# One program order for the experts of the first mixture: layers interleaved, VectorE's flags last

## The chip, the cores and the metric

The kernel runs on one core of one Trainium2 chip. The metric is device time in microseconds (us), median of the runs of a version. TensorE (PE) multiplies, VectorE (DVE) and ScalarE (ACT) do elementwise work, GpSimd (POOL) issues gathers and scatters through a table of row numbers, and SyncE (SP) issues the other transfers.

## The reference

What is computed is an attention without softmax, then two mixtures of experts (MoE), on 4608 rows of 512:

```python
kv = np.einsum('bhsd,bhse->bhde', k, v)
out = np.einsum('bhsd,bhde->bhse', q, kv)        # then a norm over each head
...
for e in range(E):                               # MoE1: 8 experts, two per row
    for k in range(2):
        mask = top2[:, k] == e
        h = np.maximum(x[mask] @ w1[e], 0.0)
        out[mask] += top2_w[mask, k, None] * (h @ w2[e])
...
do_compute = x @ w_skip > 0                      # MoE2: one expert per kept row
logits = x[do_compute] @ w_gate
...
out[do_compute] = xc + gate_w * (np.maximum(xc @ w1[e], 0.0) @ w2[e])
```

## The kernel before

Products are made from 16-bit halves: a matrix in 32 bits is scaled by a power of two and split into a high and a low part, and three products of parts stand for one.

The attention and the routing of MoE1 end some 240 us into the span. Then come the experts of MoE1. Each expert has ten tiles of 128 rows (a tile of row numbers each), and two tiles make a group, so an expert has five groups; two groups of expert 0 are done earlier, and 38 are left. Here a **slot** is the work of PE between the ends of two groups. A group is layer 1 in four pieces of 24 products (line 218, out to `hh` by ACT and `hl` by DVE, lines 226 and 227) and layer 2 for each tile (line 252, 24 products each, out to `ysb` by ACT, line 1010). The last group of an expert has 224 rows instead of 256.

A tile's result is added to the result of the row's other expert (`yo`, gathered by POOL from `ydram`, line 1001; the sum is line 1014) and scattered to `out_dram` (line 1017). It also goes into the routing of MoE2: squares (`jk`, line 867), a power of two from them, two parts (`xh`, lines 870 and 871), a transposing transfer (`x2T`, line 886), products with the gate (lines 891 and 893), some twenty small operations of DVE, ranks (lines 934 to 936), and a product that puts the row's number into its place in MoE2's tables (line 964).

Beside this, the weights of the next expert and those of MoE2 are prepared. The table `MATS` has five letters per expert, one per group: F is half of the next expert's weights (`wa`, `wb`), P is half of an expert's weights of MoE2 (`presplit`, which is then written to `wsd` in DRAM, line 1036). A matrix of 2 MB is loaded into one of two `stage` buffers (lines 187, 191), squared in four passes (`wjunk`, line 165), its sums reduced (`wsum`, line 168) and added over partitions on PE (line 171), a power of two made from it, and then split in four parts, each by ACT (line 181) and DVE (line 182).

PE's order is written by hand throughout. From group 3 to group 34 the order of the other four engines is set by the framework's scheduler, which takes instructions by its own estimate of when they are ready; before and after they run as the program is written. All DMAs that SP issues go through one queue.

After group 37 come units of MoE2: `Ra[0]`, `Ra[1]` (two units whose rows are known early) and u0, u1 and so on, whose rows come from `next_rows`, after the last group's place.

Of the kernel before, what the change touches and what calls it, by code (L numbers as in the profile page):

```python
# [15 lines left out]
P = 128  # L16
# [15 lines left out]
BEGIN = 3  # L32
# [3 lines left out]
AHEAD = [{(CUT + 2, 0): "g", (CUT + 2, 1): "a", (CUT + 3, 0): "s", (CUT + 3, 1): "b"},  # L36
         {(CUT + 3, 2): "g", (CUT + 4, 0): "s", (CUT + 4, 1): "a"}]
# [41 lines left out]
def moe_kernel(ctx: ExitStack, tc: tile.TileContext, q, k, v, g_norm, w_gate, w_noise, noise,  # L79
# [43 lines left out]
    def pow2_scale(ss_ps, kk, name):  # L123
# [5 lines left out]
        V.tensor_scalar(u[:, 0], t, -1.0, float(kk), op0=ALU.mult, op1=ALU.add)  # L129
        V.tensor_scalar(u[:, 1], t, 1.0, float(254 - kk), op0=ALU.mult, op1=ALU.add)  # L130
        s = tiny.tile([P, 2, n], I32, name=name + "s")
        V.tensor_scalar(s, u, 23, None, op0=ALU.logical_shift_left)  # L132
        f = s.bitcast(F32)
        return f[:, 0], f[:, 1]
# [21 lines left out]
    def split_matrix(load, hi, lo, scale, kk, sc, inv):  # L156
# [15 lines left out]
        a0, i0 = pow2_scale(ps, kk, "wsc")  # L172
        if scale is None:
            V.tensor_copy(sc, a0)  # L174
        else:
            V.tensor_mul(sc, a0, scale)
        V.tensor_copy(inv, i0)
# [53 lines left out]

    def layer1(W, xT, nt, point=None):
        hh = p2.tile([P, 8, 2 * P], F16, name="hh")
        hl = p2.tile([P, 8, 2 * P], F16, name="hl")
        if nt % P:
            G.memset(hh[:, :, nt:2 * P], 0.0)
            G.memset(hl[:, :, nt:2 * P], 0.0)
        for fp in range(8 * nt // 512 if nt % P == 0 else 4):
            layer1_piece(W, xT, nt, hh, hl, fp)
            if point:  # L240
                point(fp)
        return hh, hl
# [583 lines left out]


# [3 lines left out]
    racc = m1.tile([P, 1], F32, name="racc")  # L831
    rjunk = m1.tile([P, 36], F32, name="rjunk")
    A.activation(rjunk, rw.rearrange("p c n -> p (c n)"), AF.Square, accum_out=racc)
    rps = pSm[0].tile([P, 1], F32, name="small")
    PE.matmul(rps, ones32, racc, start=True, stop=True)
    rs, ri = pow2_scale(rps, 199, "rsc")
    rsk = m1.tile([P, 2], F32, name="rsk")
    V.tensor_copy(rsk[:, 0:1], rs)
    V.tensor_copy(rsk[:, 1:2], ri)
# [734 lines left out]
```

## Time and profile before

| | us |
|---|---|
| median of three runs | 1341.67 (1341.3 to 1344.72) |
| profiled execution, its time | 1338.29 |
| its span | 1336.3 |
| attention and routing, to the first slot | 243.0 |
| 38 slots of MoE1 | 243.0 to 1098.8 |
| MoE2 and the end | 1098.8 to 1336.3 |

PE is busy for 1220.6 us of the span (91%), DVE for 799.7, ACT for 667.3. The mean granted clock is 0.969. A slot can be read as a stretch of PE between the last products of one group's layer 2 and those of the next; a view that cuts the span at these ends gives each slot's length, every engine's busy time in it, the granted clock and how busy the DMA engines were.

### The profile page before, as it was taken

What the parts mean: (1) busy time and instruction counts of PE and PEld (TensorE: products, weight loads), DVE (VectorE), ACT (ScalarE), POOL (GpSimd) and SP (SyncE); (2) the same over time, 40 slices, a digit from 0 to 9 for tenths busy, and PEclk for the clock granted to TensorE, in tenths of its full rate; (3) what the DMA queues carried; (4) which work ended last, traced back from release to release, by engine and by line L of the source; (5) the groups of instructions that cost most, each with busy time, mean ns of one, the idle gap of its engine ahead of it and who ended that gap; (6) DMA issues with size and microseconds to landing.
All of it is one profiled execution on the core that took longest, in us unless ns stands there. A gap on an engine that the chain in (4) does not pass through costs nothing.

```text
span 1336.3 us, 25221 instructions
## 1 busy us (share of the span) xinstructions
PE 1220.6 (91%) x9443; PEld 866.1 (65%) x9443; DVE 799.7 (60%) x2730; ACT 667.3 (50%) x1227; POOL 388.3 (29%) x460
## 2 busy tenths in 40 slices
PE   5777789898999999999999999999999999999995
PEld 5666677565667666756666666666576766576663
DVE  1667878134585776676667766667776765433321
ACT  1569662255565656476466575647574332122210
POOL 2322332212333232423332232242312342222220
PEclk8978889998999999999999999999999999999998
DMA  9989963667985977888799797778977584677670
GB/s 239 294 241 297 310 181 86 176 196 220 262 236 164 258 259 196 238 208 266 153 287 264 255 292 242 225 202 265 304 232 225 150 211 137 198 243 224 197 225 13
DMA packets 318757, 296.30 MB, mean 222 GB/s; under 512 B 211888, under 2 KB 263088, under 8 KB 314524
## 3 DMA queue, kind: packets, MB, share of 16 engines
q1 hardware_dynamic: 294940, 210.31, 58.3%
q0 software_dynamic: 23104, 83.18, 18.5%
q8 instruction: 78, 1.28, 0.4%
q10 hardware_dynamic: 576, 1.05, 0.3%
q14 instruction: 59, 0.48, 0.1%
HBM read 174.46 MB, written 94.73 MB: 201 GB/s over the span
## 4 chain that ended last, share of the span: by engine, by line
PE 34%; DVE 19%; issue 15%; ACT 13%; DMA 12%; POOL 4%; SPq 2%; POOLq 0%; DVEq 0%; ACTq 0%
PE b L252 18%; PE a L218 10%; DMA stage<-in_moe_w_dram 8%; ACT wjunk L165 3%; DVE wb L182 2%; ACT presplit L181 2%; DVE wa L182 2%; DVE hl L227 2%; DMA xg<-xrows,idx 2%; DVE xh L871 2%; PE kvps L385 1%; PE b L450 1%; ACT hh L226 1%; ACT ysb L1010 1%; POOL out_dram L1096 1%
## 5 line engine op out<-in xcount | busy, mean ns | idle before, releaser
L218 PEld LDWEIGHTS <-wa 128*128 128x128 f16 x5184 | 474.4, 99 | 68.1 <-issue 15.4
L218 PE MATMUL a<-xT,wa 128*128 128x256 f16 (+1 forms) x3648 | 403.9, 271 | 12.9 <-DVE hl L227 10.6
L252 PE MATMUL b<-wb,hh 128*128 128x512 f16 x1536 | 352.6, 380 | 19.8 <-ACT hh L226 19.7
L252 PEld LDWEIGHTS <-hh 128*128 128x128 f16 x1536 | 144.2, 98 | 188.6 <-ACT hh L226 34.0
L226 ACT ACTIVATE hh<-a 128x512 f16<-128x512 f32 (+1 forms) x192 | 109.9, 577 | 191.1 <-PE a L218 190.8
L1017 POOL DMA_INDIRECT out_dram<-x,oi x70 | 73.1, 1045 | 430.2 <-DVE nact L946 308.2
L252 PE MATMUL b<-wb,hl 128*128 128x512 f16 x768 | 182.6, 380 | 1.9 <-DVE hl L227 1.9
L227 DVE SCALAR_TENSOR_TENSOR hl<-a,hh 128x512 f16<-128x512 f32 (+1 forms) x192 | 128.0, 674 | 77.0 <-ACT hh L226 76.9
L252 PEld LDWEIGHTS <-hl 128*128 128x128 f16 x768 | 75.2, 98 | 94.0 <-DVE hl L227 4.1
L1010 ACT ACTIVATE ysb<-b,gate 128x512 f32<-128x512 f32 x76 | 51.7, 680 | 154.3 <-PE b L252 154.3
L165 ACT ACTIVATE wjunk<-stage 128x1024 bf16<-128x1024 f32 x96 | 101.0, 1052 | 38.0 <-DMA stage<-in_moe_w_dram 36.8
L218 PE MATMUL a<-x2Tr,wa 128*128 128x256 f16 (+1 forms) x1152 | 109.2, 257 | 4.9 <-DMA x2Tr<-xh 4.5
L978 POOL DMA_INDIRECT xg<-xrows,idx x76 | 75.2, 990 | 97.3 <-DVE gate L987 58.4
L1001 POOL DMA_INDIRECT yo<-ydram,gi x70 | 77.1, 1101 | 60.9 <-issue 21.5
L182 DVE SCALAR_TENSOR_TENSOR presplit<-stage,wscl,presplit 128x1024 f16<-128x1024 f32 x64 | 80.0, 1279 | 9.5 <-ACT presplit L181 9.0
L181 ACT ACTIVATE presplit<-stage,wscl 128x1024 f16<-128x1024 f32 x64 | 70.7, 1139 | 15.3 <-DVE wscl L174 15.3
L450 PE MATMUL b<-kvbd,qTs 128*128 128x160 f32 x256 | 52.8, 346 | 21.8 <-issue 10.0
L1014 DVE TENSOR_TENSOR x<-ysb,yo 128x512 f32<-128x512 f32 x70 | 48.2, 689 | 34.5 <-ACT ysb L1010 33.6
L867 ACT ACTIVATE jk<-x 128x512 bf16<-128x512 f32 x70 | 43.9, 627 | 45.3 <-DVE x L1014 44.7
L494 POOL TENSOR_TENSOR osb<-osb,rinv 128x1024 f32<-128x1024 f32 (+1 forms) x20 | 37.2, 1862 | 86.9 <-DVE rinv L141 71.6
L450 PEld LDWEIGHTS b<-kvbd,qTs 128*128 128x128 f32 x256 | 42.7, 219 | 26.5 <-issue 10.8
L870 ACT ACTIVATE xh<-x,x2ss 128x512 f16<-128x512 f32 x70 | 46.7, 714 | 18.7 <-DVE x2ss L132 18.0
(330 smaller groups left out, 1510.6 us busy)
## 6 DMA issues: line engine op xcount, KB each, us to landing
stage<-in_moe_w_dram SPq DMA_DIRECT2D x32, 2048.0 KB, 10.4
ydram<-ysb SPq DMA_DIRECT2D x66, 256.0 KB, 5.6
wsd<-presplit SPq DMA_DIRECT2D x8, 2056.0 KB, 7.2
wsd<-presplit SPq DMA_DIRECT2D x8, 2048.0 KB, 8.9
out_dram<-zeros SPq DMA_DIRECT2D x9, 1024.0 KB, 8.1
km<-in_k_dram SPq DMA_DIRECT2D x16, 512.0 KB, 7.0
vm<-in_v_dram SPq DMA_DIRECT2D x16, 512.0 KB, 6.3
qm<-in_q_dram SPq DMA_DIRECT2D x16, 512.0 KB, 7.3
```

The source lines that it names most:

```text
L165: A.activation(junk, st[:, F * c:F * c + F], AF.Square, accum_out=acc[:, c:c + 1], **kw)
L181: A.activation(hi[:, d], st[:, d], AF.Copy, scale=sc)
L182: V.scalar_tensor_tensor(lo[:, d], st[:, d], sc, hi[:, d], op0=ALU.mult, op1=ALU.subtract)
L218: PE.matmul(ps[:, i, :], a[:, c, fs], xT[:, b + c, 0:nt], start=(n == 0), stop=(n == 11))
L226: A.activation(hh[:, fsl, 0:nt], ps, AF.Relu)
L227: V.scalar_tensor_tensor(hl[:, fsl, 0:nt], ps, 0.0, hh[:, fsl, 0:nt], op0=ALU.max, op1=ALU.subtract)
L252: PE.matmul(ps, a[:, f, gsl], b[:, f, :], start=(fs.start == 0 and i == 0), stop=(fs.stop == 8 and a is hl and f == 7))
L450: PE.matmul(po[:, i, :], qT[:, i, :], kvb[b % 4][:, h0 + i, :], start=True, stop=True)
L978: G.indirect_dma_start(out=xg[:, g], out_offset=None, in_=xrows, in_offset=bass.IndirectOffsetOnAxis(ap=idx1[:, t0 + g:t0 + g + 1], axis=0))
L1001: G.indirect_dma_start(out=yo, out_offset=None, in_=ydram[0:e * C1, :], in_offset=bass.IndirectOffsetOnAxis(ap=gi[:, g:g + 1], axis=0), bo ...
L1010: A.activation(ysb, ps, AF.Copy, scale=gate[:, g:g + 1])
L1017: s = G.indirect_dma_start(out=out, out_offset=bass.IndirectOffsetOnAxis(ap=oi[:, g:g + 1], axis=0), in_=x2[:, g], in_offset=None, bounds_ ...
```

## The change

All engines run in program order from the first slot on, and the program is written anew for it as a slot per group. Layer 1 of the next group now stands between the two halves of layer 2 of this group: two pieces, layer 2 of the first tile, two pieces, layer 2 of the second tile. The steps of the routing and of the matrices have fixed places. A matrix is loaded at the end of one slot, squared in the next and split in the one after. The flags and the gate column of a group (from its gathered rows) stand last on DVE in the slot ahead. The squares and powers of two of the second gate are made per tile instead of per group. `pow2_scale` takes three operations of DVE instead of four and writes its results where they are wanted, several other small operations go away, and the product `rhs` moves from POOL to DVE. The layer 1 of `Ra[0]` and `Ra[1]` are done in and right behind the last slot, group 37's place follows the layer 2 of `Ra[0]`, and `others` stands ahead of the splitting of u0's rows. A fallback for overfull experts at the program's end is put inside another conditional block.

```diff
+    def pow2_scale(ss_ps, kk, name, a=None, inv=None):
...
-        u = tiny.tile([P, 2, n], I32, name=name + "u")
...
+            a, inv = f[:, 0], f[:, 1]
+        V.tensor_scalar(a.bitcast(I32), t, -2.0 ** 23, kk * 2.0 ** 23, op0=ALU.mult, op1=ALU.add)
+        V.tensor_scalar(inv.bitcast(I32), t, 2.0 ** 23, (254 - kk) * 2.0 ** 23, op0=ALU.mult, op1=ALU.add)
+        return a, inv
     def log_recip_newton(r, vv, shape, name, half):
...
+    order.enter_context(tc.manual_schedule(engines={
+        mybir.EngineType.SP, mybir.EngineType.Pool, mybir.EngineType.Activation, mybir.EngineType.DVE}))
...
+        def squares(self, g, x2):
+            self.ss = tiny.tile([P, 1], F32, name="ss2")
+            jk = p2.tile([P, D], BF16, name="jk", bufs=1)
+            A.activation(jk, x2, AF.Square, accum_out=self.ss)
+            self.a = tiny.tile([P, 1], F32, name="x2a")
+            pow2_scale(self.ss, 195, "x2s", self.a, self.rsc[:, g:g + 1])
+        def parts(self, g, x2):
+            xh = self.xh
+            A.activation(xh[:, g, 0:D], x2, AF.Copy, scale=self.a)
+            V.scalar_tensor_tensor(xh[:, g, D:2 * D], x2, self.a, xh[:, g, 0:D], op0=ALU.mult, op1=ALU.subtract)
+            SP.dma_start_transpose(out=self.xT[:, :, g * P:g * P + P], in_=xh[:, g])
...
+        def flags(self):
+            aux = self.xg[:, :, 512:528]
+            e = self.e
+            if e:
+                self.fl = tiny.tile([P, 2], F32, name="fl")
+                V.tensor_scalar(self.fl, aux[:, :, 8], float(e), None, op0=ALU.is_equal)
+                nf = tiny.tile([P, 2], F32, name="nf")
+                V.tensor_scalar(nf, self.fl, -BIG, BIG, op0=ALU.mult, op1=ALU.add)
+                self.gi = tiny.tile([P, 2], I32, name="gi")
+                V.tensor_add(self.gi, aux[:, :, 9], nf)
+                self.oi = tiny.tile([P, 2], I32, name="oi")
+                V.scalar_tensor_tensor(self.oi, idx1[:, self.t0:self.t0 + 2], -1.0, nf, op0=ALU.add, op1=ALU.add)
+            self.gate = tiny.tile([P, 2], F32, name="gate")
+            V.tensor_scalar(self.gate, aux[:, :, e], Ws[e][4], None, op0=ALU.mult)
...
+        def out(self, g):
+            e = self.e
             ysb = p2.tile([P, D], F32, name="ysb", bufs=3)
-            A.activation(ysb, ps, AF.Copy, scale=gate[:, g:g + 1])
+            A.activation(ysb, self.ps, AF.Copy, scale=self.gate[:, g:g + 1])
             if e < E - 1:
-                SP.dma_start(ydram[(t0 + g) * P:(t0 + g + 1) * P, :], ysb)
+                SP.dma_start(ydram[(self.t0 + g) * P:(self.t0 + g + 1) * P, :], ysb)
             if e:
...
+    def matrix(n):
+        m = mats[n] if n < len(mats) else None
         if m is None:
             return None
         kind, e, half = m
         if half == 0:
             gens[kind] = first_weights(e, w1, w2, gcol, 0.5, Ws[e]) if kind == "first" else presplit(e)
-        return gens[kind][half]
-    engines = {mybir.EngineType.SP, mybir.EngineType.Pool, mybir.EngineType.Activation, mybir.EngineType.DVE}
-    begin = ExitStack()
-    begin.enter_context(tc.manual_schedule(engines=engines))
-    xs = {0: gather1(*groups[0])}
+        g = gens[kind][half]
+        next(g)
+        return g
...
+    def go(g, n=1):
+        for _ in range(n if g else 0):
+            next(g, None)
+    for g in groups[0:3]:
+        g.gather()
     for t in yob:
...
+    for g in groups[0:2]:
+        g.turn()
+    groups[0].flags()
+    squares = matrix(0)
+    parts = None
+    l1 = groups[0].first()
+    for i in range(4):
+        l1.matmuls()
+        l1.out()
+    prev = prev2 = Nothing()
+    for n, cur in enumerate(groups):
...
+        h = l1.h
+        l1 = groups[n + 1].first() if n + 1 < len(groups) else Layer1(Wa[0], Ra[0].xT, 2 * P)
+        l1.matmuls()
+        prev.out(1)
+        cur.others()
+        prev.scatter(1)
+        prev.squares(1)
+        l1.out()
+        l1.matmuls()
+        prev.parts(1)
+        if n + 2 < len(groups):
+            groups[n + 2].turn()
+        go(parts)
+        l1.out()
+        prev2.then("ranks")
+        cur.second(0, h)
+        go(parts)
+        prev2.then("slots")
+        go(squares)
+        go(parts)
+        go(squares)
+        ahead_work(n, 0)
+        l1.matmuls()
+        cur.out(0)
+        cur.scatter(0)
+        cur.squares(0)
+        l1.out()
+        l1.matmuls()
+        cur.parts(0)
+        ahead_work(n, 1)
+        l1.out()
+        go(parts)
+        prev2.then("place")
+        prev.then("logits")
+        cur.second(1, h)
+        if n == CUT + 2:
+            pick_early()
+        go(parts)
+        prev.then("gate")
+        ahead_work(n, 2)
+        go(squares, 2)
+        after = matrix(n + 1)
+        if n == 0:
+            prepare()
+        if n + 3 < len(groups):
+            groups[n + 3].gather()
+        if n + 1 < len(groups):
+            groups[n + 1].flags()
+        prev, prev2 = cur, prev
+        parts, squares = squares, after
+    l1s = [l1, Layer1(Wa[1], Ra[1].xT, 2 * P)]
+    l1 = l1s[1]
+    l1.matmuls()
+    prev.out(1)
+    prev.scatter(1)
+    prev.squares(1)
+    l1.out()
+    l1.matmuls()
+    prev.parts(1)
+    prev2.then("ranks")
+    prev2.then("slots")
+    l1.out()
+    for i in range(2):
+        l1.matmuls()
+        l1.out()
+    prev2.then("place")
...
+    def step(k):
+        if k == 0:
+            prev.then("logits")
+            prev.then("gate")
+        elif k == 1:
+            prev.then("ranks")
+            prev.then("slots")
+        else:
+            prev.then("place")
+            next_rows()
+            for _ in range(2):
+                stream.pop(0).gather(osc2)
+    moe2_unit(Wa[0], Ra[0], step, h=l1s[0].h)
+    def step(k, f=later(-1)):
+        if k == 1:
+            others()
+            f(0)
+        if k:
+            f(k)
+    moe2_unit(Wa[1], Ra[1], step, h=l1s[1].h)
     for u in range(len(units)):
...
-    with flag(NX // 2):
...
+        with flag(NX // 2):
```

Three engines at the places that matter follow, each as the order of instructions before and then after.

ACT before, in the second slot of expert 2 (`wa` is the split of next weights, `wjunk` the squares of the matrix loaded meanwhile, `rdf` the exponential of the gate):

```order
L867 ACTIVATE jk,ss_5298<-x_5140 128x512
L226 ACTIVATE hh<-a 128x512
L870 ACTIVATE xh<-x_5140,x2ss 128x512 x2
L181 ACTIVATE wa<-stage,wscl 128x1024
L226 ACTIVATE hh<-a 128x512
L181 ACTIVATE wa<-stage,wscl 128x1024 x2
L226 ACTIVATE hh<-a 128x512
L181 ACTIVATE wa<-stage,wscl 128x1024
L165 ACTIVATE wjunk,wacc<-stage 128x1024
L226 ACTIVATE hh<-a 128x512
L165 ACTIVATE wjunk,wacc<-stage 128x1024 x3
L1010 ACTIVATE ysb<-b,gate 128x512
```

ACT after, from the middle of the same slot to its end:

```order
L177 ACTIVATE wa<-stage,wscl 128x1024
L164 ACTIVATE wjunk,wacc<-stage 128x1024
L177 ACTIVATE wa<-stage,wscl 128x1024
L164 ACTIVATE wjunk,wacc<-stage 128x1024
L1074 ACTIVATE ysb<-b,gate 128x512
L908 ACTIVATE jk,ss_5548<-x_5397 128x512
L222 ACTIVATE hh<-a 128x512
L914 ACTIVATE xh<-x_5397,x2a 128x512
L222 ACTIVATE hh<-a 128x512
L177 ACTIVATE wa<-stage,wscl 128x1024 x2
L941 ACTIVATE rdf<-rdf 128x16
L164 ACTIVATE wjunk,wacc<-stage 128x1024 x2
```

The four squares stood behind the four splits and ran in one go; now two stand between the first splits, and two behind the last splits and the exponential.

SP before, about the first slot of expert 2 (`wsd` is the write of a split matrix of MoE2, `stage` a load, `x2T` and `xT` transposing transfers):

```order
L1012 DMA ydram<-ysb 128x512 x2
L886 DMA_TRANSPOSE x2T<-xh 128x8x128 x2
L980 DMA_TRANSPOSE xT<-xg 128x8x128 x2
L1036 DMA wsd_2801<-presplit 128x8192
L1012 DMA ydram<-ysb 128x512
L191 DMA stage<-in_moe_w_dram 128x8x512
L1012 DMA ydram<-ysb 128x512
L886 DMA_TRANSPOSE x2T<-xh 128x8x128 x2
```

SP after, at the end of that slot:

```order
L1037 DMA_TRANSPOSE xT<-xg 128x8x128 x2
L1076 DMA ydram<-ysb 128x512
L916 DMA_TRANSPOSE x2T<-xh 128x8x128
L1113 DMA wsd_2792<-presplit 128x8192
L187 DMA stage<-in_moe_w_dram 128x8x512
L1076 DMA ydram<-ysb 128x512
L916 DMA_TRANSPOSE x2T<-xh 128x8x128
L1037 DMA_TRANSPOSE xT<-xg 128x8x128 x2
L1076 DMA ydram<-ysb 128x512
L916 DMA_TRANSPOSE x2T<-xh 128x8x128
```

The load stood behind the write and a `ydram` write; now it stands right behind the `wsd` write, at the end of the slot, with a slot's transfers behind both. Such a pair, write and load, stands at ten places of SP's order.

PE before, in a slot with a matrix (line 218 is layer 1):

```order
L218 LDWEIGHTS wa
L218 MATMUL a<-xT,wa 128x256
L218 LDWEIGHTS wa
L218 MATMUL a<-xT,wa 128x256
L171 MATMUL small<-wsum,ones_72 128x1
L218 LDWEIGHTS wa
L218 MATMUL a<-xT,wa 128x256
L218 LDWEIGHTS wa
L218 MATMUL a<-xT,wa 128x256
```

PE after, in such a slot (line 264 is layer 2; lines 978 to 980 are ranks):

```order
L214 LDWEIGHTS wa
L214 MATMUL a<-xT,wa 128x256
L170 MATMUL small<-wsum,ones_72 128x1
L978 LDWEIGHTS tri_74
L978 MATMUL small<-rm_4085,tri_74 128x16
L979 LDWEIGHTS ones_70
L979 MATMUL small<-rm_4085,ones_70 128x8
L980 LDWEIGHTS ones_70
L980 MATMUL small<-c_2810,ones_70 128x16
L264 LDWEIGHTS hh
L264 MATMUL b<-wb,hh 128x512
L264 LDWEIGHTS hh
```

The sum of the squares was added between two pieces of layer 1; now it stands behind the slot's second piece, ahead of layer 2 of the first tile.

## Rows read from the trace of the kernel before

**Rows 1.** The page's chain that ended last, by line:

```profile
PE b L252 18%; PE a L218 10%; DMA stage<-in_moe_w_dram 8%; ACT wjunk L165 3%; DVE wb L182 2%; ACT presplit L181 2%; DVE wa L182 2%; DVE hl L227 2%; DMA xg<-xrows,idx 2%; DVE xh L871 2%; PE kvps L385 1%; PE b L450 1%; ACT hh L226 1%; ACT ysb L1010 1%; POOL out_dram L1096 1%
```

**Rows 2.** Slots: bounds, length, busy PE, PEld, DVE, ACT, POOL, clock, DMA share, GB/s.

```profile
407.90:428.20 20.30, 20.28 (x169) 14.45 (x166) 10.78 (x49) 10.50 (x21) 5.02 (x6) 1.00 0.55 122
428.20:449.80 21.60, 21.60 (x171) 14.87 (x170) 15.78 (x58) 10.57 (x17) 9.51 (x9) 1.00 0.85 201
...
807.00:832.70 25.70, 23.48 (x172) 15.61 (x171) 16.30 (x59) 14.48 (x25) 6.24 (x7) 0.93 0.70 227
...
sum 855.80, PE 818.42 PEld 558.20 DVE 558.59 ACT 486.68 POOL 257.29; mean PE 21.54 PEld 14.69 DVE 14.70 ACT 12.81 POOL 6.77
```

**Rows 3.** Groups on PE, 235 to 1130 us: count, busy and mean, idle before, releaser.

```profile
L218 PE MATMUL a<-xT,wa 128*128 128x256 f16 (+1 forms) x3648 | 403.9, 271 | 12.9 <-DVE hl L227 10.6 <-DMA xT<-xg 2.1
L252 PE MATMUL b<-wb,hh 128*128 128x512 f16 x1248 | 286.5, 379 | 17.6 <-ACT hh L226 17.5
...
L171 PE MATMUL small<-wsum,ones 128*128 128x1 f32 x60 | 9.0, 218 | 6.7 <-DVE wsum L168 6.7
```

**Rows 4.** Groups on ACT, 340 to 1100 us, same columns.

```profile
L165 ACT ACTIVATE wjunk<-stage 128x1024 bf16<-128x1024 f32 x84 | 88.4, 1053 | 37.8 <-DMA stage<-in_moe_w_dram 36.8
L226 ACT ACTIVATE hh<-a 128x512 f16<-128x512 f32 (+1 forms) x136 | 77.0, 572 | 19.8 <-PE a L218 19.6
L181 ACT ACTIVATE presplit<-stage,wscl 128x1024 f16<-128x1024 f32 x60 | 66.3, 1139 | 9.1 <-DVE wscl L174 9.1
L1010 ACT ACTIVATE ysb<-b,gate 128x512 f32<-128x512 f32 x69 | 46.9, 680 | 133.8 <-PE b L252 133.8
...
L165 ACT ACTIVATION_READ_ACCUMULATOR wjunk<-stage 128x1 f32 x84 | 16.0, 190 | 0.0
```

**Rows 5.** Groups on DVE, 340 to 1100 us, same columns.

```profile
L182 DVE SCALAR_TENSOR_TENSOR presplit<-stage,wscl,presplit 128x1024 f16<-128x1024 f32 x60 | 75.0, 1279 | 8.0 <-ACT presplit L181 7.5
...
L1014 DVE TENSOR_TENSOR x<-ysb,yo 128x512 f32<-128x512 f32 x69 | 47.5, 689 | 32.1 <-ACT ysb L1010 31.2 <-issue 0.3
```

**Rows 6.** SP's timeline, 824 to 900 us: start, duration, what.

```profile
825.18 0.33 SPq L1036 DMA_DIRECT2D wsd<-presplit  x1
...
892.09 0.53 SPq L1036 DMA_DIRECT2D wsd<-presplit  x1
```

**Rows 7.** DMAs issued from 828.3 to 828.9 us, with us to landing.

```profile
stage<-in_moe_w_dram SPq DMA_DIRECT2D x1, 2048.0 KB, 12.8
```

**Rows 8.** DMAs issued from 893.8 to 894.4 us, with us to landing.

```profile
stage<-in_moe_w_dram SPq DMA_DIRECT2D x1, 2048.0 KB, 16.1
```

**Rows 9.** The tile of loads, 340 to 1100 us, its transfers.

```profile
DMA to landing us min/median/max: 8.0/10.7/16.1
```

**Rows 10.** The written matrices, 340 to 1100 us, their transfers.

```profile
DMA to landing us min/median/max: 6.7/8.2/9.0
```

**Rows 11.** POOL's timeline at the start of expert 7, idle time before in brackets.

```profile
1000.09 1.07 POOL L1001 DMA_INDIRECT yo<-ydram,gi  x1 [6.82 <-DMA x2T<-xh]
```

**Rows 12.** PE's timeline from MoE1 into MoE2, same columns.

```profile
1123.24 0.30 PE L964 MATMUL idx2ps<-rhs,ohp 128*128 128x160 f16 x2
...
1136.21 1.89 PE L252 MATMUL b<-wb,hh 128*128 128x512 f16 x4 [2.19 <-ACT hh L226]
...
1145.57 10.64 PE L218 MATMUL a<-x2Tr,wa 128*128 128x256 f16 x96
...
1168.85 1.36 PE L218 MATMUL a<-x2Tr,wa 128*128 128x256 f16 x11 [2.28 <-DMA x2Tr<-xh]
```

**Rows 13.** Chain of waits, 1100 to 1180 us: start, us, what.

```profile
1135.70 0.75 DVE xh L871
...
1142.10 0.20 DVE tot L1356
```

**Rows 14.** Instructions of the last conditional's check, line 1427.

```profile
L1427 POOLq TENSOR_LOAD <-fli x2: 307/404/500, 1321.2 to 1326.6; - x2
```

**Rows 15.** Instructions of the program's end, line 1570.

```profile
L1570 POOLq DRAIN  x3: 40/107/5377, 1330.0 to 1336.0; - x3
```

More of the change, by code (lines that the diff above doesn't have):

```diff
@@ L1021, in moe1_group, with scatter @@
-            step(1 + g)
-            point(4 + 2 * g)
-            point(5 + 2 * g)
-        return finalize(e, i0, xg, x2, fl) if e else None
+                V.tensor_add(self.x2[:, g], ysb, yob[(self.t0 + g) % 4])
+        def scatter(self, g):
+            if not self.e:
+                return
+            G.memset(spacer, 0.0)
+            s = G.indirect_dma_start(out=out, out_offset=bass.IndirectOffsetOnAxis(ap=self.oi[:, g:g + 1], axis=0),
+                                     in_=self.x2[:, g], in_offset=None, bounds_check=N - 1, oob_is_err=False)
+            nodep(s.ins, osc + rd2, "rows of other tokens")
+            osc.append(s.ins)
@@ L1026, in presplit, with squares, parts, then @@
+        def squares(self, g):
+            if self.e:
+                if g == 0:
+                    self.fin = Finish(self.e, self.i0, self.fl)
+                self.fin.squares(g, self.x2[:, g])
+        def parts(self, g):
+            if self.e:
+                self.fin.parts(g, self.x2[:, g])
+        def then(self, what):
+            if self.e:
+                getattr(self.fin, what)()
     def presplit(e):
@@ L1168, in pick_early @@
             ahead.append(cols)
-    groups = [(e, i0) for e in range(E) for i0 in range(0, T1, 2)][EARLY // 2:]
     Ws = {0: W0}
+    groups = [Group(e, i0) for e in range(E) for i0 in range(0, T1, 2)][EARLY // 2:]
     mats = list(MATS[EARLY // 2:])
@@ L1198, in moe_kernel, with __getattr__ @@
+    class Nothing:
+        def __getattr__(self, name):
+            return lambda *a: None
+    Ra, Wa = [], ([], [])
+    NF0 = (T1 - EARLY) // 2
+    def go(g, n=1):
[3 more added lines that the diff above has]
+        g.gather()
     for t in yob:
         G.memset(t, 0.0)
[L1200 to L1242 removed]
@@ L1375, in split @@
             r.split()
-    def point(p):
-        if p == 0:
-            next(fin, None)
-            next_rows()
-            for _ in range(2):
-                stream.pop(0).gather(osc2)
-        elif p == PB:
-            split(-1)
     def later(u):
@@ new lines, in moe_kernel @@
+                sec = Second(1, p3.tile([P, 8, 2 * P], F16, name="x2Tr"))
+                sec.squares(0, xg[:, 0:D])
+                sec.parts(0, xg[:, 0:D])
+                sec.logits()
+                act, oh, gt = sec.gates(one)
+                g = tiny.tile([P, 2], F32, name="gate")
+                V.tensor_mul(g[:, 0:1], act, gt)
+                V.tensor_scalar(xg[:, D:D + 8], oh[:, 0], g[:, 0:1], None, op0=ALU.mult)
+                SP.dma_start(x2d[bass.ds(j, P), :], xg[:, 0:D + 8])
```

489 lines of the change are left out of this document (213 added, 276 removed).

## The prediction

> **What bounds the kernel now.** I read three views in this order. The page's chain shows which work ended last: products of the two layers lead (18% and 10%), and right behind them stands the load of a matrix into `stage` (8%) with the squares and splits that hang on it [rows 1]. So TensorE bounds MoE1, and what stops it comes from ACT, DVE and the loads. The slot view then says how much that is. A slot in which nothing is late takes 21.6 us and PE is busy in all of it; one of the 224-row groups takes 20.3 [rows 2]. Thirty slots of 21.6 and eight of 20.3 make 810.4 us, and the 38 slots take 855.8: **45.4 us** above an undisturbed run. The groups on PE say where PE stood: 17.6 us ahead of layer 2 for the last `hh` of its own layer 1, 12.9 ahead of layer 1 (10.6 for `hl`, which frees the buffers), 6.7 at the sum of a matrix's squares [rows 3]: 37.2 us. The other 8 or so are PE busy, but at the low clock: the slot at 807 holds a stall of 2.2 us (25.70 less 23.48 busy), its granted clock is 0.93, and PE is busy in it for 23.48 us instead of 21.6, so a stall of this size costs another 1.9.
>
> DMA engines are busy for about half of a light slot (0.55) and 0.85 of the undisturbed full one [rows 2]: they are no bound, but a transfer has to wait its turn.
>
> **What the change takes away.** In the new order a whole tile of layer 2 (5.2 us) and two later pieces stand between a piece of layer 1 and the layer 2 that reads it. The 17.6 us for `hh` are covered by that; a late `hh` has to be later than some 5 us to show again. The sums of squares are made a slot before PE asks, and the flags no longer stand ahead of DVE work that PE waits for. I take the whole 45.4 us away as the most there is: a slot cannot go below 21.6, since no product is removed.
>
> The smaller DVE edits (one power-of-two operation less, copies gone, `rhs` moved from POOL) I cost at nothing: DVE is busy for 15.8 of 21.6 us even in a slot without stalls [rows 2], so these operations lie beside PE. Without that cover, two fewer per slot at some 0.2 us and one more `rhs` are worth less than 0.5 us either way, on work that ends a slot early.
>
> **What it adds: a ring through load, squares and split.** Times are counted from the start of a slot of 21.6 us. A piece of layer 1 takes 10.64/4 = 2.66 us [rows 12], so the fourth piece ends at 5.3 + 5.2 + 5.3 + 0.3 = 16.1. Behind it ACT has the relu (0.57), then the last two splits (1.14 each), and DVE ends its half of the last one 1.28 later [rows 4, 5]: 20.3. Only then is the `stage` buffer free and the split matrix whole, and SP issues the write to `wsd` and, right behind it, the load. With T from the write's issue to the load's landing, the load lands at 20.3 + T - 21.6 = T - 1.3 of the next slot. ACT meets it there at the first square, with all its later work queued behind: three splits, `ysb`, two squares of rows, two relus, `xh`, the exponential, three squares. In a row that is four squares with their readout (4 x 1.24), three splits (3.4), five passes over 512 columns of 0.57 to 0.68 (3.2), DVE's addition (0.69), DVE's last split (1.28) and some six small operations of 0.19 (1.2): 14.7 us [rows 4, 5]. PE asks for the sum at 21.6 + 5.3 = 26.9. So **PE waits T - 1.3 + 14.7 - 26.9 = T - 13.5 us**, at the ten places where a write stands right ahead of a load. Without a write the load lands after 8.0 us at best and 10.7 in the median [rows 9], and PE waits for nothing.
>
> T is not in the trace as such. The nearest rows are loads that followed a write after 2 to 3 us: 825.18 to 828.3 + 12.8 = 841.1, that is 15.9, and 892.09 to 893.8 + 16.1 = 909.9, that is 17.8 [rows 6 to 8]; of six such loads these are the earliest and the second latest. From below, the fastest write and the fastest load one after the other make 6.7 + 8.0 = 14.7 [rows 9, 10], and if they overlap in part, 13.5 or less and no wait. By SP's order two transposing transfers stood just ahead of the write then and 256 KB of `ydram` between; in the new order neither is there. I take T = 15.5, a little under the lower row, and keep 13.5 and 17.8 as ends.
>
> The Trainium skill ("DMA: Bandwidth & Descriptors", section "Queues, rings and completion order") says that SP owns one ring on each of the DMA engines and that descriptors in a ring are consumed in order. By that the load does not start until the write's descriptors are through, and T is a sum; the landings of 15.9 and 17.8 against 10.7 agree. Were the two served side by side, T would be 10.7 and none of the ten places would wait.
>
> So with T = 15.5: ten waits of 2.0 us make 20. A wait of 2.2 brought the low clock [rows 2]; at 2.0 I count a third of 1.9, 0.6 each: 6. Five of the places (in experts 4 to 6, where such slots follow each other closely) begin with splits already late by about 1: 5.5. At the start of experts 5 and 7, POOL's gather of `yo` waits for a `ydram` write that stands in SP's queue behind the pair, and the addition, two relus and two splits behind it wait too. At expert 7 of before POOL stood 6.8 us there [rows 11], under cover; I count 2 each, 4 (0 to 8).
>
> **Around it.** `pick_early` comes last in its slot on DVE, and its slot's ranks wait: 2. At the **transition**, group 37's place came at 1123.24 and u0 started at 1145.57 without waiting [rows 12]; from the place to u0's split was 13.2 us (1136.45), and `others` took till 1142.3, some 5 us behind it [rows 13]. In the new order `others` stands ahead of the split, so u0's rows are there 16 to 21 us behind the place, while PE has only the second layer of `Ra[1]` in between, 10.4 us. PE waits 6 to 10 and pays 2 of clock. In return go the stalls of 2.19 and 2.28 with their slow clock [rows 12], about 8 together. Net -1 to +8; I take 2.6. At the **end**, POOL reads a second flag from 1326.6 and jumps, and the last drain starts at 1330.0 [rows 14, 15]. With the fallback inside the other block, check and jump go: -3.4.
>
> **The sum.** 1338.3 (profiled execution) - 45.4 + 20 + 6 + 5.5 + 4 + 2 + 2.6 - 3.4 = 1329.6. The median of the runs lies 3.4 above the profiled one: **1333 us**.
>
> **Rivals.** *Waits hidden*: write and load overlap, T is at or under 13.5. The 35.5 us of the ring are gone and the median is some 1298 to 1308 with a few small stalls left. For it speaks that the queue is emptier there; against it that none of the six loads behind a write landed so early. *The ring eats the gain (slower)*: the same mechanism with T as the rows have it. At T = 16.9, their middle, each of ten waits is 3.4, and 1.9 of clock comes with each: 53; the late splits of the close places 8, `yo` 5; 66 in place of 35.5, so 1363; at 17.8 it is 9 more for the waits and some 6 for the close places, 1378. It decides from about T = 16.2, where 2.7 + 0.7 at ten places and 10 beside them make up for all that was removed. For it speak both rows, against it the emptier queue. *It does not do what it says*: with four engines in a fixed order, small waits on DVE or ACT take the place of those removed and slots stay at 22.5; then the median is within a few us of 1341. Against it: only 15.8 us of DVE and 10.6 of ACT are busy in a slot at 21.6 [rows 2].
>
> **Chances.** About 0.3% (4 us) is what a measurement of this kernel can tell from no change. Forecast (1320 to 1344): 0.42, of which 0.33 is faster by more than that and 0.09 within it. Waits hidden: 0.20, faster. The ring eats the gain: 0.31, slower. It does not do what it says: 0.07, 0.06 of it the same, 0.01 slower. Faster 0.53, same 0.15, slower 0.32. The range leaves out half of the hidden case and a third of the slower one: **1303 to 1364**.
>
> **What would show it.** Right: idle time ahead of layer 2 for `hh` gone; most slots 21.6; waits of 1 to 3 us at the product of `wsum` two slots behind each of the ten pairs, and the chain there through load, `wjunk`, splits and `wjunk` again; loads behind a write landing 15 to 16 us after the write's issue, about 14 into a slot; a wait ahead of u0's layer 1; a POOL without second flag load. Wrong: loads landing under 13 or over 17; waits at `hl` or the rows' logits instead; slots without a write that are longer than 22.

## The result, and the profile after

The changed kernel takes **1357.1 us** (median of six runs, 1352.1 to 1367.2), the kernel before 1344.6 beside it (1341.3 to 1347.8): ratio **1.011**, 95% interval 1.008 to 1.014. The time lies inside the range of the prediction, but the forecast was faster, and the kernel is slower by 1.1%. The profiled execution took 1365.6 us (span 1363.7), 8.5 above the median; a second one, below, lies 4.8 under the median of its own run.

The page's chain of the changed kernel by line, which answers to [rows 1]:

```profile
PE b L264 17%; PE a L214 16%; DMA stage<-in_moe_w_dram 10%; DMA x2T<-xh 4%; ACT wjunk L164 3%; DVE presplit L178 3%; ACT hh L222 2%; PE b L462 1%; ACT presplit L177 1%; PE kvps L397 1%; DVE wa L178 1%; POOL out_dram L1174 1%; DMA ydram<-ysb 1%; DVE x L1078 1%; ACT xh L914 1%
```

`hh`, `wb` and `hl` no longer stand near its head; the load has grown, and `x2T` (the transposing load that brings a slot's rows to the second gate) is new, with 4%.

To see where the time is, I cut both spans at the same four points of TensorE's program: the last sum of the first routing, the first product of u0, the last product, the end. Windows of the kernel before (bounds, length, busy PE, PEld, DVE, ACT, POOL, clock, DMA share, GB/s):

```profile
0.00:240.54 240.54, 187.78 (x1539) 162.62 (x1540) 159.74 (x407) 131.75 (x293) 75.42 (x93) 0.89 0.85 234
240.54:1145.57 905.03, 863.14 (x6561) 587.72 (x6560) 586.79 (x2180) 498.16 (x860) 267.77 (x296) 0.99 0.79 225
1145.57:1319.90 174.33, 169.67 (x1345) 115.78 (x1343) 52.45 (x142) 37.42 (x74) 44.13 (x72) 0.99 0.67 206
1319.90:1336.30 16.40, 0.00 (x0) 0.00 (x0) 0.75 (x1) 0.00 (x0) 0.98 (x1) 0.62 0.05 14
```

And of the changed kernel:

```profile
0.00:246.65 246.65, 193.53 (x1539) 166.16 (x1540) 158.60 (x393) 131.35 (x291) 76.19 (x93) 0.87 0.85 233
246.65:1176.75 930.10, 867.36 (x6561) 592.10 (x6560) 600.45 (x2099) 500.44 (x862) 255.38 (x328) 0.97 0.84 219
1176.75:1350.60 173.85, 170.21 (x1344) 116.13 (x1344) 49.63 (x127) 37.08 (x74) 41.85 (x68) 0.99 0.65 203
1350.60:1363.70 13.10, 0.00 (x1) 0.00 (x0) 0.75 (x1) 0.00 (x0) 0.98 (x1) 0.69 0.04 13
```

Differences: +6.1 up to the first mixture (3.4 of it a wait for `hhe` at 239, 1.7 the slow products behind it, the rest spread over the attention), **+25.1** in it, -0.5 behind it, -3.3 at the end. The products are the same (6561 in the stretch of the mixture); 20.9 of the 25.1 are PE standing idle and 4.2 a lower clock. The groups on PE in that stretch up to 1141 us say for whom, as [rows 3] did before (count, busy and mean, idle before, releaser):

```profile
L214 PE MATMUL a<-xT,wa 128*128 128x256 f16 (+1 forms) x3648 | 400.1, 270 | 0.0
L264 PE MATMUL b<-wb,hh 128*128 128x512 f16 x1216 | 288.1, 392 | 0.0
...
L924 PE MATMUL small<-rw,x2T 128*128 128x18 f16 x272 | 16.0, 172 | 38.7 <-DMA x2T<-xh 38.7
...
L170 PE MATMUL small<-wsum,ones 128*128 128x1 f32 x60 | 9.5, 228 | 13.0 <-DVE wsum L167 13.0
L978 PE MATMUL small<-rm,tri 128*128 128x16 f16 x33 | 5.6, 170 | 3.7 <-DVE rm L966 3.7
```

Everything that [rows 3] showed ahead of both layers is gone. What is new stands at three products: the second gate's logits for `x2T`, 38.7 us; the sums of squares, 13.0; the ranks, 3.7. Five of the waits on PE's timeline, the last of them at u0 (start, duration, idle before in brackets):

```profile
729.19 0.28 PE L924 MATMUL small<-rw,x2T 128*128 128x18 f16 x4 [3.73 <-DMA x2T<-xh]
...
958.64 0.26 PE L924 MATMUL small<-rw,x2T 128*128 128x18 f16 x4 [4.03 <-DMA x2T<-xh]
...
1016.87 0.38 PE L170 MATMUL small<-wsum,ones 128*128 128x1 f32 x2 [2.56 <-DVE wsum L167]
...
1103.93 0.28 PE L924 MATMUL small<-rw,x2T 128*128 128x18 f16 x4 [26.92 <-DMA x2T<-xh]
...
1176.75 3.59 PE L214 MATMUL a<-x2Tr,wa 128*128 128x256 f16 x16 [7.33 <-DMA x2Tr<-xh]
```

The fourth alone is 26.9 us, more than the whole difference in the mixture (25.1). The changed kernel's chain of waits names the transfer, and, in the first row, an ordinary load behind a write:

```profile
987.30 14.15 DMA stage<-in_moe_w_dram
...
1070.06 33.83 DMA x2T<-xh
```

SP's timeline: a write and a load, then, at the long wait, `x2T` of slot 36, then `x2Tr` (the transposing load of the first row unit):

```profile
986.92 0.33 SPq L1113 DMA_DIRECT2D wsd<-presplit  x1
987.30 0.46 SPq L187 DMA_DIRECT2D stage<-in_moe_w_dram  x1
...
1070.06 1.33 SPq L916 DMA_TRANSPOSE x2T<-xh  x1
1075.22 31.60 SPq L1158 DMA_TRANSPOSE x2Tr<-xh  x2
```

And POOL's, which gathers the two halves of the first row unit's weights, 2 MB each:

```profile
1065.42 0.97 POOL L1124 DMA_INDIRECT wa<-wsd,ewi  x1 [0.30 <-PE small L980]
...
1071.24 0.97 POOL L1124 DMA_INDIRECT wb<-wsd,ewi  x1 [0.30 <-issue]
```

`x2T` was issued between the two gathers, and the two instructions of `x2Tr` behind it kept SP for 31.6 us (the first alone for 19.2). What the DMA engines did in the middle of it, 1080 to 1090 (q0 carries POOL's gathers, q1 SP's transfers: packets, MB, share of 16 engines):

```profile
DMA packets 434, 0.78 MB, mean 78 GB/s; under 512 B 383, under 2 KB 383, under 8 KB 395
...
q0 software_dynamic: 59, 0.69, 73.0%
q1 hardware_dynamic: 375, 0.09, 53.3%
```

In the kernel before such a gather ran by itself, 1078 to 1083:

```profile
DMA packets 148, 2.11 MB, mean 423 GB/s; under 512 B 18, under 2 KB 18, under 8 KB 20
...
q0 software_dynamic: 148, 2.11, 98.7%
```

The gather moves at 78 GB/s instead of 423, while packets of the two queues are under way the whole time (73.0 and 53.3% of the engines' time, and they overlap). In the records of single packets it lasts from 1076.4 to 1103.3, 26.9 us instead of 5.0, beside 1044 packets of 256 bytes of the transposing loads, which average 248 ns instead of the 18 that they take alone. So the theory to test: **a gather and transposing loads hold each other up**. The rival: `x2T` is late for the reason forecast for the loads, the ring behind the squares' writes, or through chance of one execution.

### The profile page after: what moved, and what is told of

The parts are those of the page before. It is cut to its first block, busy times and chain, and to the rows that moved or that the text cites. A ratio compares the mean times of both kernels' runs of the same rounds, so it can differ in the third digit from the quotient of the medians.

```text
span 1363.7 us, 25101 instructions
## 1 busy us (share of the span) xinstructions
PE 1231.1 (90%) x9443; PEld 874.4 (64%) x9443; DVE 809.4 (59%) x2620; ACT 668.9 (49%) x1227; POOL 374.4 (27%) x489
## 4 chain that ended last, share of the span: by engine, by line
PE 38%; DMA 17%; issue 16%; DVE 12%; ACT 12%; POOL 3%; SPq 1%; another core or an unknown queue 1%; POOLq 0%; DVEq 0%; ACTq 0%
PE b L264 17%; PE a L214 16%; DMA stage<-in_moe_w_dram 10%; DMA x2T<-xh 4%; ACT wjunk L164 3%; DVE presplit L178 3%; ACT hh L222 2%; PE b L462 1%; ACT presplit L177 1%; PE kvps L397 1%; DVE wa L178 1%; POOL out_dram L1174 1%; DMA ydram<-ysb 1%; DVE x L1078 1%; ACT xh L914 1%
## 5 line engine op out<-in xcount | busy, mean ns | idle before, releaser
L264 PE MATMUL b<-wb,hh 128*128 128x512 f16 x1536 | 360.4, 390 | 0.0
L264 PEld LDWEIGHTS <-hh 128*128 128x128 f16 x1536 | 147.9, 100 | 170.7 <-issue 17.7
L1063 POOL DMA_INDIRECT yo<-ydram,gi x70 | 84.8, 1212 | 276.9 <-DVE gate L1056 149.0
L178 DVE SCALAR_TENSOR_TENSOR wa<-stage,wscl,wa 128x1024 f16<-128x1024 f32 x32 | 40.4, 1283 | 41.4 <-ACT wa L177 40.7
```

What stands on the lines that cost most here:

```text
L178: V.scalar_tensor_tensor(lo[:, d], st[:, d], sc, hi[:, d], op0=ALU.mult, op1=ALU.subtract)
L264: PE.matmul(ps, a[:, f, gsl], b[:, f, :], start=(fs.start == 0 and i == 0), stop=(fs.stop == 8 and a is hl and f == 7))
L1063: G.indirect_dma_start(out=yob[(self.t0 + g) % 4], out_offset=None, in_=ydram[0:e * C1, :], in_offset=bass.IndirectOffsetOnAxis(ap=self.gi ...
```

## The experiments

**The same kernel again.** No edit.

> The changed kernel once more, as the base for the others. Its executions so far lie between 1352 and 1367 us. If the stall of 26.9 us ahead of the gate's products near the end of the first mixture is a collision of transfers, its length should differ from execution to execution and be the larger part of that spread; if it is a fixed chain of instructions, it should be 26 to 28 us again. The stall of 3.4 us ahead of the first slot: again there if it comes from the order of instructions, gone if it was chance.

1357.7 us (1353.0 to 1366.0), ratio 1.009 (1.005 to 1.013). The stall is there again in PE's timeline, in an execution of 1353.0, but shorter, so it is no fixed chain of 26 to 28 us:

```profile
1097.70 0.28 PE L924 MATMUL small<-rw,x2T 128*128 128x18 f16 x4 [19.14 <-DMA x2T<-xh]
```

The start of the mixture differs: instead of the first profile's 3.4 us for `hhe`, PE waits 4.8 us there for `xT`.

**One gather moved.** The second half of the first row unit's weights is gathered two places later. (In these diffs the table's keys are slot and place, CUT + 3 written as 36; "a" and "b" are the gathers of the two halves, "s" is `x2Tr`, "g" the rows.)

```diff
-         (36, 0): ((0, "s"), (0, "b")), (36, 1): ((1, "g"),),
+         (36, 0): ((0, "s"),), (36, 1): ((1, "g"),), (36, 2): ((0, "b"),),
```

> Only the gather of the second half of the weights of the first known unit is moved, from the middle of slot 36 to its end, about 10 us later on POOL. Theory (the gather of 2 MB and the transposing transfer of the rows for the gate are in flight together and hold each other up): the stall ahead of the gate's products falls from 26.9 to under 4 us, the time by 15 to 25 us to about 1335. Rival (pick_early, late on DVE, makes everything behind it late): the stall stays over 15 us and the time within 5 us of 1357.

1356.1 us (1344.3 to 1359.2), ratio 1.008 (1.004 to 1.012). In the profiled execution, which was the fastest with 1344.3, the stall is down to 3.4 us; the median hardly moves, where about 1335 was expected. The next run but one shows where it went.

**The load ahead of the write.** The squares' matrix is written to `wsd` one step later, so that SP issues the next `stage` load first.

```diff
+            yield
             SP.dma_start(wsd[n][e * P:(e + 1) * P, :], t[:, 0:WB if n else WA])
...
         after = matrix(n + 1)
+        go(parts)
```

> Only the order on SP at the ends of slots is changed: the load of the next matrix stands ahead of the write of the split one. Theory (the ring through load, squares and split): the waits for the sums of squares, together with those for the rows' transposes in slots 3 to 34 some 21 us, fall to under 8 (two places where a split has to wait for the write before it remain), the slow clock that follows them falls too, and the time falls by 15 to 28 us to about 1335. Rival (squares and splits are late by their order on ACT and DVE, whenever the load lands): the waits and the time stay within 5 us.

1346.5 us (1344.8 to 1353.3), ratio 1.001 (0.998 to 1.003): 11 us less than the changed kernel. Its groups on PE from 246 to 1141:

```profile
L924 PE MATMUL small<-rw,x2T 128*128 128x18 f16 x280 | 16.3, 172 | 34.6 <-DMA x2T<-xh 34.6
...
L1011 PE MATMUL idx2ps<-rhs,ohp 128*128 128x160 f16 x68 | 10.4, 235 | 6.7 <-DVE ohp L1005 6.7
L170 PE MATMUL small<-wsum,ones 128*128 128x1 f32 x60 | 8.6, 213 | 0.4 <-DVE wsum L167 0.4
```

The wait at the sums of squares (line 170) is down from 13.0 us to 0.4. So the ring that the prediction describes is real, and its repair is worth 11 us net (15 to 28 were expected), since 6.7 us of waiting for `ohp` come up in its place. PE's timeline has the stall still:

```profile
1092.61 0.28 PE L924 MATMUL small<-rw,x2T 128*128 128x18 f16 x4 [22.77 <-DMA x2T<-xh]
```

The other waits for `x2T` add up to 11.8 us, as in the changed kernel. The rival, the ring behind the squares' writes, falls as the cause of the stall: it stands here with the load first, and in the changed kernel the last such write was issued at 1034.1, 36 us ahead of this `x2T`.

**Both together.**

> Both edits. If the two causes are separate, the gains add up: 35 to 50 us under the changed kernel, 1307 to 1322. If they share a cause (DMA traffic that only moves elsewhere), much less than the sum.

1346.2 us, ratio 0.998 (0.994 to 1.002), with executions from 1334 to 1353: no lower than the load first alone. PE's timeline in the profiled one, of 1350.3:

```profile
1113.89 0.28 PE L924 MATMUL small<-rw,x2T 128*128 128x18 f16 x4 [20.10 <-DMA x2T<-xh]
```

The stall has moved one slot on. There a gather of the second row unit's `wa` now follows the displaced `wb` closely; by its packets it lasted 23.8 us. The same placement stood in the run with one gather moved; that its slower executions had this stall is likely, but they left no trace.

**Gathers spaced.** From the changed kernel, both second halves go behind the last slot.

```diff
-         (36, 0): ((0, "s"), (0, "b")), (36, 1): ((1, "g"),), (37, 0): ((1, "s"), (1, "a")), (37, 2): ((1, "b"),)}
+         (36, 0): ((0, "s"),), (36, 1): ((1, "g"),), (37, 0): ((1, "s"), (1, "a"))}
...
     prev.scatter(1)
+    dyn_weights(ewi[:, 0:1], 0, Wa[0], 1)
...
         if k == 0:
+            dyn_weights(ewi[:, 1:2], 2, Wa[1], 1)
```

> Edit: the changed kernel, with only the places of the four early weight gathers moved, so that none stands beside more than one transposing load of the second MoE (x2T of a slot or x2Tr of a row tile): the second half of each matrix is gathered one place later. Theory A (a gather of 16 KB packets and two transposing loads queued together hold each other up, some 20 us): the gap ahead of the logits of slot 36 (26.9 us in the first profile, 19.1 in the second) is under 5 us, no gather lasts over 11 us, and the median falls from 1357 to 1333 to 1343 with a smaller spread between runs than the kernel with one gather moved. Rival B (the transposing loads are late for another reason, such as the ring behind the squares' writes): a gap of over 15 us stays somewhere between 1060 and 1130, and the median stays at 1350 or above.

1350.8 us (1345.4 to 1358.1), ratio 1.003 (0.999 to 1.007): 7 less than the changed kernel, not the 14 or more expected. No gather is slow. But the two second halves stand directly behind each other now, the `x2T` issued beside them lands 14.5 us later, and PE waits 8.6 us for it and 7.3 at u0.

**Is it two transposing loads?** `x2Tr`, issued 4 us behind the gather, is moved one place later.

```diff
-         (36, 0): ((0, "s"), (0, "b")), (36, 1): ((1, "g"),),
+         (36, 0): ((0, "b"),), (36, 1): ((0, "s"), (1, "g")),
```

> Edit: the changed kernel, the weight gather left where it is (slot 36, place 0, with x2T of the slot), but x2Tr of the row tile, issued four microseconds behind it, moved one place later. Theory A1 (it takes the gather and two transposing loads at once): the gather lasts 6 to 11 us and the gap ahead of the logits of slot 36 is under 6 us. Rival A2 (the gather and one transposing load are enough when the load is issued first): the gap stays at 15 to 27 us.

One execution, 1358.8 us. PE's timeline:

```profile
1100.05 0.28 PE L924 MATMUL small<-rw,x2T 128*128 128x18 f16 x4 [20.17 <-DMA x2T<-xh]
```

My version of the theory falls: `x2Tr` is not needed. The gather still lasts 19.1 us. That one transposing load is enough is not shown, though, since SP's timeline has the slot's second `x2T` in the middle of it:

```profile
1083.22 7.26 SPq L916 DMA_TRANSPOSE x2T<-xh  x1
```

From 1080 to 1084, ahead of that, the gather started 50 of its 128 packets, half the pace of the undisturbed one (128 in 5.0 us); from 1085 to 1093 it started 14.

**Is it two gathers?** Every weight gather gets a place of its own. The first one stands where the second one stood, between the same `x2T` and `x2Tr`, with no gather in progress ahead of it.

```diff
-    (35, 2): ((0, "g"), (0, "a")), (36, 0): ((0, "s"), (0, "b")), (36, 1): ((1, "g"),),
-    (37, 0): ((1, "s"), (1, "a")), (37, 2): ((1, "b"),)
+    (35, 2): ((0, "g"),), (36, 0): ((0, "s"), (0, "a")), (36, 1): ((1, "g"),), (36, 2): ((0, "b"),),
+    (37, 0): ((1, "s"),), (37, 1): ((1, "a"),), (37, 2): ((1, "b"),)
```

> Edit: the changed kernel with each early weight gather at a place of its own: the first one is not issued ahead of slot 36 but in its place 0, where the second one stood, between x2T of the slot and x2Tr of the row tile; the others follow one place apart. So a gather meets the same two transposing loads as in the changed kernel, but no other gather is in progress when they are issued. Theory B1 (the stall takes two gathers close behind each other with a transposing load issued between them): no gather above 11 us, the gap ahead of the logits of slot 36 is under 6 us, median 1338 to 1350. Rival B2 (one gather that starts over a transposing load in progress is enough): the gap of 15 to 27 us is still there, and the median stays at 1350 to 1360.

**1340.1 us** (1336.6 to 1341.4), ratio 0.995 (0.993 to 0.997): 17 us less than the changed kernel, by one table (19 to 21 by the ratios to the kernel before, which took 1346.0 beside it). Groups on PE from 238 to 1120, then the DMA queue of the gather from 1072 to 1080:

```profile
L924 PE MATMUL small<-rw,x2T 128*128 128x18 f16 x272 | 15.7, 171 | 8.9 <-DMA x2T<-xh 8.9
...
L170 PE MATMUL small<-wsum,ones 128*128 128x1 f32 x60 | 9.8, 233 | 13.1 <-DVE wsum L167 13.1
```

```profile
DMA packets 675, 2.25 MB, mean 282 GB/s; under 512 B 534, under 2 KB 534, under 8 KB 549
...
q0 software_dynamic: 159, 2.13, 81.9%
```

The gather runs at 282 GB/s over 534 small packets: together with a transposing load, but without a gather close ahead, it is not slow. The ring's 13.1 us are untouched, as they should be. The table has a price: layer 1 of the first row unit now waits 3.5 us for `x2Tr`, and that of the second 2.5 for its gathered weights.

**The same in the kernel before.** There the second gather is issued 7 to 10 us earlier, close behind the first.

```diff
-AHEAD = [{(35, 0): "g", (35, 1): "a", (36, 0): "s", (36, 1): "b"},
+AHEAD = [{(35, 0): "g", (35, 1): "a", (35, 2): "b", (36, 0): "s"},
```

> Edit: the kernel before, with one table entry moved: the second gather of the first matrix is issued about 7 us earlier, close behind the first one and just behind x2T of slot 36, instead of behind x2Tr of the row tile. Theory B1 (two gathers close behind each other with transposing loads issued between and beside them hold each other up): that gather lasts 12 to 27 us instead of 5.0, TensorE has a gap of over 8 us between 1065 and 1100, and the median goes up by 8 to 20 us. Rival (it takes something that only the new order has): the gather stays under 9 us, no new gap, the median within 3 us of the kernel before.

> Edit: none against the kernel before with its second gather issued close behind the first; a second profiled execution of it. In the first profile, of its fastest execution (1345.7 us, where the median was 1352.3), both gathers ran at full speed and no gap stood at them: x2T was issued 0.7 us behind the second gather, not between the two. Theory B1 (the slow gather needs the transposing load issued between the two): again gathers of 6 to 7 us, no gap over 4 us between 1060 and 1110, and what makes the median longer lies elsewhere (the start of the first MoE had a gap of 6.1 and one of 5.6 us in the first profile). Rival (the pair of gathers alone is enough, in most executions): a gather of 12 us or more and a gap of over 8 us between 1065 and 1110.

1352.3 us (1345.7 to 1364.6), ratio 1.007 (1.003 to 1.011), 10 us more. But neither expectation is confirmed by that: in neither profile (1345.7 and 1353.7 us) is a gather slow (6.0 and 7.9 us). The DMA queue of the first from 1070 to 1076:

```profile
q0 software_dynamic: 171, 2.15, 91.9%
q1 hardware_dynamic: 490, 0.13, 10.7%
```

`x2T` was issued 1.7 us behind the second gather, not between the two, and waited for it: PE stood for 2.2 us in one and 6.1 in the other. So the order of the changed kernel, with `x2T` between the two, was not made here, and what the rest of the 10 us is stays open.

**All repairs.** Five edits: the load first; gathers spaced as above; `pick_early` ahead of the slot's last layer 2; the third group's gather behind the first tile's layer 1; `f(0)` ahead of `others`.

```diff
-    for g in groups[0:3]:
+    for g in groups[0:2]:
         g.gather()
...
         l1.out()
+    groups[2].gather()
...
-        cur.second(1, h)
         if n == CUT + 2:
             pick_early()
+        cur.second(1, h)
...
         if k == 1:
-            others()
             f(0)
+            others()
```

> Edit: the changed kernel with five repairs at once: the stage load issued ahead of the squares' write; the weight gathers spaced as in the run on spacing; the early pick ahead of the slot's second PSUM half instead of behind it; the third group's gather behind the first tile's layer 1; the later row tiles' work of the first unit behind the split of its own tile. If the losses read from the trace add up: load first -11, the stall -20, the early pick -4 to -5 (3.7 of waiting and 1.7 of clock), the start -2 to -4 (the gap near 245 falls from 4.8 to under 2), the wait ahead of u0 -4 to -5 (7.3 to about 2): 1357 less 41 to 45 is 1312 to 1316, 2% below the kernel before. If the stall is only half there on average, or the collision moves to another gather again: 1322 to 1335. If the repairs hide one another: 1335 to 1346, no better than load first with one gather moved.

1329.5 us (1323.9 to 1339.6), ratio 0.990 (0.987 to 0.994): what was expected if the collision moves to another gather. Of the waits on PE, the one for `x2T` behind the pair of gathers, 7.7 us, is the largest. One of the two was then moved a step later:

```diff
         if k == 0:
-            dyn_weights(ewi[:, 1:2], 2, Wa[1], 1)
             prev.then("logits")
             prev.then("gate")
         elif k == 1:
+            dyn_weights(ewi[:, 1:2], 2, Wa[1], 1)
```

> Edit: the kernel with all repairs, in which the second halves of the two matrices were gathered directly behind each other (slot 37's x2T, issued 0.5 us behind the second, was late: a gap of 7.7 us at 1103); now the last gather is issued one step of the first row unit later. Theory B1 (a transposing load issued behind a gather waits for it, and behind two for both): the gap at 1103 falls to under 2 us, nothing else moves, median 1320 to 1325. Rival: the wait moves on to the layer 2 that reads the later gather (a gap ahead of the second row tile's layer 2), median 1326 to 1331.

1329.8 us (1323.7 to 1334.2), ratio 0.988 (0.984 to 0.991). The wait for `x2T` fell to 2.4, and 5.5 us appeared ahead of the layer 2 that reads the later gather: the rival named there, a wait that moves on.

**Single gathers and the four other repairs.** The table as in "Is it two gathers?", the other edits as in "The load ahead of the write" and "All repairs".

> Edit: the changed kernel with single gathers (each early weight gather at a place of its own) and the four other repairs: the stage load ahead of the squares' write, the early pick ahead of the second PSUM half, the third group's gather behind the first tile's layer 1, the row unit's later tiles behind its own split. If the losses add up: 1340 less 11 (loads first), 4 to 5 (pick, with its clock), 2 to 4 (start) and 3 to 5 (u0) is 1315 to 1320, ratio 0.977 to 0.981. Rival (the gathers meet other transposing loads again, since the repairs move SP's and POOL's order by several us): 1325 to 1335, like the other kernel with all repairs.

**1319.3 us** (1316.8 to 1329.9), ratio **0.983** (0.974 to 0.991), inside what was expected: this version beats both kernels. Its groups on PE from 238 to 1150:

```profile
L214 PE MATMUL a<-xT,wa 128*128 128x256 f16 (+1 forms) x3648 | 400.1, 270 | 1.8 <-DMA xT<-xg 1.8
...
L214 PE MATMUL a<-x2Tr,wa 128*128 128x256 f16 x288 | 35.5, 289 | 10.5 <-DMA x2Tr<-xh 7.8 <-DMA wa<-wsd,ewi 2.7
L924 PE MATMUL small<-rw,x2T 128*128 128x18 f16 x280 | 16.3, 171 | 9.1 <-DMA x2T<-xh 9.1
...
L1011 PE MATMUL idx2ps<-rhs,ohp 128*128 128x160 f16 x70 | 10.7, 236 | 6.8 <-DVE ohp L1005 6.8
```

And its windows from the routing to u0:

```profile
239.05:1125.91 886.86, 858.64 (x6562) 590.64 (x6560) 598.35 (x2078) 504.57 (x862) 256.40 (x328) 0.99 0.86 230
```

Against the kernel with single gathers alone the four repairs bring 21 us (17 by the ratios): waits at the sums 13.1 less, for which 6.8 come at `ohp`; at the start 4.3 became 1.8; at the ranks 4.1 became nothing; PE is busy 7 us less in the mixture, at a higher clock. At u0 the repair did little: 7.3 became 4.2, and u1 waits 4.1 instead of 2.2.

## Why the prediction was wrong, step by step

- **What is removed (-45.4): right.** Nothing waits ahead of either layer, and slots without a matrix wait run at full speed. With it the mixture of the last kernel takes 886.9 us instead of 905.0, in spite of 28.2 us in it in which PE still stands (886.86 less 858.64).
- **The ring: mechanism right, 29 instead of 35.5.** Ten pairs of write and load have T from 14.5 to 15.7, mean 15.2 (986.92 to 987.30 + 14.15 = 1001.45 in the rows is the 14.5); 15.5 was forecast. PE waits 13.0 at the sums where 20 were taken. The 4 taken for `yo` and the 5.5 for the close places do not show as waits of their own; in their place PE waits 8.6 (0.8, 3.7, 4.0) for an `x2T` that stands behind such a pair on SP's queue, which the prediction had among the signs of being wrong ("waits at `hl` or the rows' logits"). The clock costs 7.5 instead of 6, but in four places: behind waits of 2.2 to 4.0 us the 24 products of a tile took 7.0 to 7.7 us (granted clock 0.69 to 0.76) instead of 5.3, behind waits of up to 1.7 they took 5.3 (1.00). The Trainium skill ("DMA: Bandwidth & Descriptors", section "Queues, rings and completion order") has descriptors of one ring consumed in order; T against a median of 10.7 for the loads of before, and the end of the waits at the sums once the load stands first, agree.
- **`pick_early`: 5.4 instead of 2** (3.7 of waiting, 1.7 of clock).
- **The transition: the wait right, the return too large.** u0 waits 7.3 (6 to 10 forecast) and pays 2.3 of clock (2 forecast). But of the two stalls that were to go in return only the one of 2.19 is gone; behind u0 the stretch is just 0.5 shorter, and u2 waits 1.9 where u1 waited 2.3.
- **The end: right**, -3.3 of -3.4.
- **The step that failed is one that has no term: the gathers of `AHEAD`.** "What it adds" costs the loads and the writes that the change moves on SP's queue, but not the weight gathers that it moves on POOL's: the first two come as a pair 5.8 us apart (18.3 before), with `x2T` between them. They were costed at nothing. In the first profile this is 26.9 + 2.8 of clock, in the second 19.1; giving each gather its own place brings 17 us of the median back. Without this stall the forecast's 1333 would have been some 7 too low (1340.1), and the sign right.
- **The start: the second missing term.** The gathers of six tiles stand up front now, the first tiles' transfers come later, and instead of the 2.1 us of [rows 3] (`xT`) the wait is 3.4 to 6.2; with the third group's gather behind layer 1 it is 1.6 to 1.9.

The rival "the ring eats the gain" named the right sign and the wrong cause: T never reached its 16.2, and the kernel with single gathers has the whole ring (13.1 us at the sums) and is still faster than before. The range reaches up to the measured time on account of this rival, so that the time lies inside it is luck.

## What to carry to other kernels

When an order is rewritten, write down every queue that a moved step passes, for each engine that issues DMAs, and ask of each large transfer what is in flight beside it; the one queue left out here cost some 17 us of the median, enough to turn a gain into a loss. Give large gathers places of their own, and let no small transfer that the matrix engine waits for be issued between two of them. Put the load that the next step needs ahead of a write that nobody waits for.

## What the runs showed of the hardware that was not expected

A gather in packets of 16 KB and a transposing load in packets of 256 bytes can slow each other to a fraction: 78 GB/s in place of 282 to 423, and an `x2T` that otherwise lands 3 to 15 us after its issue lands after 26 to 34. The slow gather is not slow in every packet: in the first profile 114 of its 128 took under 0.7 us, like the undisturbed ones (0.613), and 13 took 4 to 13 us, 111 us of engine time together. Of the 1044 packets of the transposing loads beside it 726 took under 0.1 us, 160 some 0.62, the time of one undisturbed gather packet, and 66 some 1.23, the time of two. The Trainium skill ("DMA: Bandwidth & Descriptors", section "Queues, rings and completion order") says that a DMA engine takes turns between the queues it has work for, a packet at a time. The 0.62 us would fit that; the 1.23 us and the gather's own fall to a quarter or less do not follow from it, and no run here explains them.

In all five profiles with a slow gather (26.9, 18.1, 24.4, 23.8 and 19.1 us) it was the second of two issued 5 to 6 us apart, and `x2T` was issued 1.2 to 1.7 us ahead of it. The two kernels with single gathers had none above 8.8. But the pattern is not enough by itself: the profiled execution of the kernel with one gather moved had it too, at slot 37 (5.6 us apart, `x2T` 1.2 ahead of the second), and its gather took 6.2 us. Nor is a closer pair slow: in the kernel with spaced gathers and in both with single ones the last two gathers were issued 1.3 us apart all the same, with `x2T` 0.1 to 0.2 us ahead of the second, and took 6.0 to 7.0 us. What tips it over stays open. It may be a matter of chance from one execution to the next: the ten executions of the kernel with both edits lie between 1334 and 1353, the six of the one with single gathers between 1336.6 and 1341.4. That is not shown, since the four of the last kernel, which has single gathers too, spread over 13 us (1316.8 to 1329.9).
